# The first product of a second layer by seven half-depth products instead of eight

## The chip, the cores and the metric

One core of one Trainium2 chip. Its engines work side by side, each through its own list of instructions in order: TensorE (PE: matmuls; PEld: its weight loads), VectorE (DVE), ScalarE (ACT), GpSimd (POOL) and SyncE (SP), whose queue issues the DMAs. The metric is the device time of one execution in microseconds (us), lower is better.

## The reference

Pooled attention feeds a gated layer, and that a second layer with the Mish function; everything is float32.

```python
x = attention(q, pool(k), pool(v))                  # 2304 tokens x 512
x = (sigmoid(x @ w_gate) * (x @ w_val)) @ w_out     # 512 -> 1536 -> 512
h = x @ w_in                                        # 512 -> 2048: the product that is changed
g = h * np.tanh(np.log1p(np.exp(h)))                # Mish
return g @ w_out2                                   # 2048 -> 512
```

## The kernel before

Every float32 operand of a matmul is split into a high part (a cast to the matmul's type) and a low part (operand minus high part). A product is then three matmuls: high x high, high x low, low x high (`mm3`, lines 98 to 101). All matmuls accumulate over the depth in PSUM, 128 rows at a time, in eight banks.

The first layer runs over five blocks of 512, 384, 384, 512 and 512 tokens, and in each over twelve pieces `f` of the inner width: `pg`, `pv` (products with the gate and the value weights), sigmoid and multiplication, and one piece later the `acc` matmuls with `wo`. Beside them lie the attention of the next block and the conversion of weights: they come as 64-bit numbers, a ScalarE step and three VectorE steps (`conv_scale` line 137, `conv_bits` lines 146 to 150) make float32 of them, and `conv_parts` casts on ScalarE and subtracts on GpSimd (line 160). `step` and `w2_step` say when. Of the second layer's 32 weight tiles eight are converted early and stored in DRAM as parts (`fin_w2`), 24 in the last block, into the places of first-layer weights that are done. `finish` splits a block's result into parts (lines 513 and 514) and stores both.

The second layer (lines 645 to 708) goes over the same blocks and, in each, over 16 pieces `f` of 128 inner columns. `h_unit` makes `ph` with four depth steps of `mm3` (12 matmuls), then Mish twice on ScalarE (lines 673 and 674: once in float32, once as the high part) and one subtraction on VectorE (line 675). `out_unit` follows two pieces later (`LAG`): for each 128 tokens three matmuls of 512 columns into `acc` (line 689). When a block ends its four or three `acc` banks are copied and stored.

The program's text is the order: each engine gets its instructions as they are written, nothing is rescheduled. An instruction waits by semaphores for its inputs and for the last readers of a tile whose place it takes.

## Time and profile before

| | |
|---|---|
| median of 3 runs | 952.81 us (951.9 to 953.5) |
| the profiled execution | 950.78 us, its span 949.0 us |
| TensorE (PE) busy | 917.7 us, 97% of the span, 4708 matmuls |
| VectorE (DVE) busy | 396.1 us, 42% |
| ScalarE (ACT) busy | 349.0 us, 37% |
| GpSimd (POOL) busy | 142.2 us, 15% |
| chain that ended last | PE 84%, DVE 10%, issue 3%, ACT 1%, DMA 1% |
| mean granted clock of TensorE | 0.991 |
| DMA | 114.04 MB, 120 GB/s over the span |

Busy shares are averages over the span. A matmul's duration in the trace overlaps that of the next, so its pace is the distance of two starts. An idle time is listed before the instruction that ended it, with what released it.

### The profile page before, as it was taken

What the parts mean: (1) busy time and instruction counts of PE and PEld (TensorE: products, weight loads), DVE (VectorE), ACT (ScalarE), POOL (GpSimd) and SP (SyncE); (2) the same over time, 40 slices, a digit from 0 to 9 for tenths busy, and PEclk for the clock granted to TensorE, in tenths of its full rate; (3) what the DMA queues carried; (4) which work ended last, traced back from release to release, by engine and by line L of the source; (5) the groups of instructions that cost most, each with busy time, mean ns of one, the idle gap of its engine ahead of it and who ended that gap; (6) DMA issues with size and microseconds to landing.
All of it is one profiled execution on the core that took longest, in us unless ns stands there. A gap on an engine that the chain in (4) does not pass through costs nothing.

```text
span 949.0 us, 12208 instructions
## 1 busy us (share of the span) xinstructions
PE 917.7 (97%) x4708; PEld 794.1 (84%) x4708; DVE 396.1 (42%) x651; ACT 349.0 (37%) x832; POOL 142.2 (15%) x144
## 2 busy tenths in 40 slices
PE   6889779999999999999999999999999999999998
PEld 6767658999999988888888888888888888999997
DVE  6999996533364343332687741112112111111111
ACT  5644455434355554344443342122122121222221
POOL 5567451020021100000133310000000000000000
PEclk9999899999999999999999999999999999999999
DMA  7577564633474362243765563003002100300000
GB/s 254 166 226 248 178 194 147 205 108 106 169 230 135 123 211 100 89 138 122 275 223 195 179 231 124 1 1 134 1 0 74 37 1 1 112 1 0 34 1 34
DMA packets 39610, 114.04 MB, mean 120 GB/s; under 512 B 4480, under 2 KB 6528, under 8 KB 39552
## 3 DMA queue, kind: packets, MB, share of 16 engines
q1 hardware_dynamic: 39552, 113.26, 35.1%
q8 instruction: 37, 0.61, 0.3%
q14 instruction: 21, 0.17, 0.1%
HBM read 88.60 MB, written 24.64 MB: 119 GB/s over the span
## 4 chain that ended last, share of the span: by engine, by line
PE 84%; DVE 10%; issue 3%; ACT 1%; DMA 1%; SPq 0%; DVEq 0%; ACTq 0%
PE acc L689 21%; PE ph L99 7%; PE ph L101 7%; PE ph L100 7%; PE acc L99 4%; PE acc L100 4%; PE pg L352 4%; PE acc L101 4%; PE pv L352 4%; PE pg L353 4%; PE pg L356 4%; PE pv L353 4%; PE pv L356 4%; DVE cv L147 4%; DVE cv L146 2%
## 5 line engine op out<-in xcount | busy, mean ns | idle before, releaser
L689 PE MATMUL acc<-w,g 128*128 128x512 f32 x864 | 209.8, 390 | 0.0
L689 PEld LDWEIGHTS acc<-w,g 128*128 128x128 f32 x864 | 161.7, 188 | 32.2
L675 DVE TENSOR_TENSOR g<-q,g 128x512 fp32r<-128x512 f32 (+1 forms) x80 | 51.1, 639 | 324.3 <-ACT g L674 324.3
L673 ACT ACTIVATE q<-ph 128x512 f32<-128x512 f32 (+1 forms) x80 | 44.5, 556 | 296.9 <-PE ph L101 296.9
L101 PE MATMUL ph<-x,w 128*128 128x512 f32 (+1 forms) x320 | 117.9, 368 | 0.0
L99 PE MATMUL ph<-x,w 128*128 128x512 f32 (+1 forms) x320 | 117.8, 368 | 0.0
L100 PE MATMUL ph<-x,w 128*128 128x512 f32 (+1 forms) x320 | 117.7, 368 | 0.0
L99 PE MATMUL acc<-gh,wo 128*128 128x512 f32 (+1 forms) x240 | 91.3, 381 | 1.1 <-ACT gh L617 1.1
L100 PE MATMUL acc<-gl,wo 128*128 128x512 f32 (+1 forms) x240 | 89.8, 374 | 2.3 <-POOL gl L489 1.1
L352 PE MATMUL pv<-xh,wv 128*128 128x512 f32 (+1 forms) x232 | 86.9, 375 | 3.8 <-DVE sg L614 3.8
L101 PE MATMUL acc<-gh,wo 128*128 128x512 f32 (+1 forms) x240 | 89.0, 371 | 0.0
L614 DVE TENSOR_TENSOR sg<-sg,pv 128x512 f32<-128x512 f32 (+1 forms) x58 | 36.4, 628 | 125.1 <-PE pv L356 112.2
L352 PE MATMUL pg<-xh,wg 128*128 128x512 f32 (+1 forms) x232 | 87.0, 375 | 0.6 <-ACT sg L608 0.5
L353 PE MATMUL pv<-xl,wv 128*128 128x512 f32 (+1 forms) x232 | 85.6, 369 | 0.0
L353 PE MATMUL pg<-xl,wg 128*128 128x512 f32 (+1 forms) x232 | 85.3, 368 | 0.0
L617 ACT CAST gh<-sg 128x512 fp32r<-128x512 f32 (+1 forms) x60 | 34.7, 578 | 124.7 <-DVE sg L614 124.6
L100 PEld LDWEIGHTS ph<-x,w 128*128 128x128 f32 x320 | 60.1, 188 | 8.9
L150 DVE SCALAR_TENSOR_TENSOR cv<-raw,cv 128x512 uint32<-128x512 uint32 x68 | 66.5, 978 | 2.3
L99 PEld LDWEIGHTS ph<-x,w 128*128 128x128 f32 x320 | 60.1, 188 | 8.8
L101 PEld LDWEIGHTS ph<-x,w 128*128 128x128 f32 x320 | 60.0, 188 | 7.5
L608 ACT ACTIVATE sg<-pg 128x512 f32<-128x512 f32 (+1 forms) x58 | 32.0, 552 | 90.3 <-PE pg L356 90.1
L147 DVE SCALAR_TENSOR_TENSOR cv<-raw,cv 128x512 uint32<-128x512 uint32 x68 | 62.0, 911 | 2.3
(90 smaller groups left out, 1313.1 us busy)
## 6 DMA issues: line engine op xcount, KB each, us to landing
wo<-wod SPq DMA_DIRECT2D x48, 512.0 KB
raw<-w2i SPq DMA_DIRECT2D x16, 512.0 KB
raw<-w2o SPq DMA_DIRECT2D x16, 512.0 KB
raw<-wg SPq DMA_DIRECT2D x12, 512.0 KB
raw<-wv SPq DMA_DIRECT2D x12, 512.0 KB
raw<-wo SPq DMA_DIRECT2D x12, 512.0 KB
wod<-wo SPq DMA_DIRECT2D x12, 512.0 KB
x<-x2d SPq DMA_DIRECT2D x12, 512.0 KB
```

Of the source, the lines that this page charges most:

```text
L99: nc.tensor.matmul(ps, wt[:, 0, cols], xh, start=start, stop=False)
L100: nc.tensor.matmul(ps, wt[:, 0, cols], xl, start=False, stop=False)
L101: nc.tensor.matmul(ps, wt[:, 1, cols], xh, start=False, stop=stop)
L147: nc.vector.scalar_tensor_tensor(out=c, in0=hi, scalar=0x80000000, in1=c, op0=ALU.bitwise_and, op1=ALU.bitwise_or)
L150: nc.vector.scalar_tensor_tensor(out=c, in0=lo, scalar=29, in1=c, op0=ALU.logical_shift_right, op1=ALU.bitwise_or)
L352: nc.tensor.matmul(ps[:, c0:c1], w, xh[:, k, c0:c1], start=(k == 0), stop=False)
L353: nc.tensor.matmul(ps[:, c0:c1], w, xl[:, k, c0:c1], start=False, stop=False)
L356: nc.tensor.matmul(ps[:, c0:c1], w, xh[:, k, c0:c1], start=False, stop=(k == KD - 1))
L614: nc.vector.tensor_mul(out=sg, in0=sg, in1=pv[:, :n])
L673: nc.scalar.activation(out=q, in_=ph[:, :n], func=AF.Mish)
L675: nc.vector.tensor_sub(out=g[:, 1, :], in0=q, in1=f32(g[:, 0, :]))
L689: nc.tensor.matmul(acc[t], g[:, a, c], w[:, b, :], start=(f == 0 and first), stop=(f == NF2 - 1 and last),)
```

## The change

The product `h = x @ w_in` is cut into two by two: the tokens into pairs of groups of 384 (three pairs of 768), the depth of 512 into halves, the inner width into pairs of pieces `f1`, `f2`. Each two by two product, eight half-depth products before, is made by seven (Strassen's scheme in Winograd's form): sums and differences of the x quarters and of the weight quarters are formed first, and the results are combined after.

- `prep_x2` makes, for each token pair and each of two depth steps, seven operands in parts (ScalarE: 7 casts; VectorE: 11 operations of 384 columns). The operands of the next token pair are made in the second half of a token pair, those of the first in the last block of the first layer.
- `prep_w` makes for each weight pair (2 x 512 columns, reloaded from DRAM for every token pair) four weight tiles in parts: 8 operations on VectorE, 4 casts on ScalarE.
- `product` is one of the seven: six matmuls of 384 columns into a PSUM bank, then the sums that read it. Five banks take turns, three hold `acc`.
- Of the four results of a weight pair, two (first token group) go through Mish and `parts` into `out_unit` one weight pair later; two (second group, `g2`) are kept in SBUF, and all sixteen are put through `out_unit` after the loop over weight pairs.
- The spilled weights are the unsplit float32 halves, all 16 `w_in` tiles; their conversion is spread over blocks 3 and 4 (every 4 steps instead of 8), and the 16 tiles of the output weights follow in the last block. `finish` stores x unsplit.

```diff
@@ prep_x2, prep_w
+            return [
+                [hi(1, b11), hi(2, b21)],
+                [lo(1, b11), sub(b11, b12, b11), hi(3, b22), hi(5, b11)],
+                [lo(2, b21), lo(3, b22), sub(b12, b22, b12), hi(7, b12)],
+                [lo(5, b11), sub(b22, b22, b11), hi(6, b22)],
+                [lo(7, b12), sub(b21, b21, b22), hi(4, b21)],
+                [lo(6, b22)],
+                [lo(4, b21)],
+            ]
...
+                    lambda: A.copy(out=w1[:, 0, :], in_=c1),
+                    lambda: V.tensor_sub(out=c2[:, a], in0=c1[:, a], in1=c2[:, a]),
+                    lambda: A.copy(out=w2[:, 0, :], in_=c2),
...
+                    lambda: V.tensor_sub(out=w1[:, 1, :], in0=c1, in1=f32(w1[:, 0, :])),
+                    lambda: V.tensor_sub(out=w2[:, 1, :], in0=c2, in1=f32(w2[:, 0, :])),
+                    lambda: V.tensor_sub(out=h2, in0=h2, in1=c2[:, a]),
+                    lambda: A.copy(out=w4[:, 0, a], in_=h2),
+                    lambda: V.tensor_add(out=c1[:, a], in0=c1[:, a], in1=h2),
+                    lambda: V.tensor_sub(out=c1[:, b], in0=c1[:, b], in1=h2),
+                    lambda: A.copy(out=w3[:, 0, :], in_=c1),
...
+                    lambda: V.tensor_sub(out=w4[:, 1, a], in0=h2, in1=f32(w4[:, 0, a])),
+                    lambda: V.tensor_sub(out=w3[:, 1, :], in0=c1, in1=f32(w3[:, 0, :])),
...
@@ finish, step
-                    nc.scalar.copy(out=xh[:, m, :n], in_=acc[m][:, :n])
-                    nc.vector.tensor_sub(out=xl[:, m, :n], in0=acc[m][:, :n], in1=f32(xh[:, m, :n]))
...
+                    copy((nc.scalar, nc.vector)[m % 2], x, acc[m][:, :n])
...
-                    elif i % 8 == 2 and pos2["c"] < n2:
+                    elif i % 4 == 1 and pos2["c"] < NF2:
...
@@ last block of the first layer
+                    prep = dict(enumerate(prep_x2(0), 7))
...
+                        if k == 15:
+                            load_x2(0, 1)
+                            prep.update(enumerate(prep_x2(1), 18))
...
@@ second layer: parts, the loop over weight pairs
+                    nc.scalar.activation(out=g[:, 0, :], in_=hi_from, func=AF.Mish)
+                    nc.scalar.activation(out=src, in_=hi_from, func=AF.Mish)
+                nc.vector.tensor_sub(out=g[:, 1, :], in0=src, in1=f32(g[:, 0, :]))
...
+                    def product(k, *reads):
+
+                        ps, home = bank(f"p{k}")
+                        part, c0 = PART[k]
+                        for kk in range(2):
+                            xh, xl = top[k, kk]
+                            c = slice(c0 + 128 * kk, c0 + 128 * kk + 128)
+                            mm3(ps[:, :NG], wt[part], c, xh, xl, kk == 0, kk == 1)
+                        for out, in0 in reads:
+                            if in0 is None:
+                                nc.scalar.copy(out=out, in_=ps[:, :NG])
+                            else:
+                                nc.vector.tensor_add(out=out, in0=in0, in1=ps[:, :NG])
+                        banks.append(home)
+
+                    product(1, (a, None))
+                    product(6, (u, a))
+                    product(5, (v, u))
+                    product(7, (g2[f2], v), (u, u))
+                    nc.scalar.activation(out=g2[f2], in_=g2[f2], func=AF.Mish)
+                    if n + 1 < NFP * NPR:
+                        run_all(prep_w(ws_of.pop(n + 1), w_sets[(i + 1) % 2]))
+                        if n + 3 < NFP * NPR:
+                            load_ws(n + 3)
+                    for acc_, f, g in pend:
+                        out_unit(acc_, f, g)
...
+                    product(2, (a, a))
+                    pend.append((acc, f1, parts(a, a)))
+                    product(3, (g2[f1], v))
+                    nc.scalar.activation(out=g2[f1], in_=g2[f1], func=AF.Mish)
+                    product(4, (u, u))
+                    pend.append((acc, f2, parts(u, u)))
...
@@ the second token group of a pair
+                gs = {0: parts(g2[0])}
+                out_unit(acc2, 0, gs.pop(0))
+                for n, (acc_, f, g) in enumerate(pend):
+                    out_unit(acc_, f, g)
+                    gs[n + 1] = parts(g2[n + 1])
+                evict(acc, o)
+                pend = []
+                for f in range(1, NF2):
+                    if p + 1 < NPR and f >= NF2 - 2:
+                        pend.append((acc2, f, gs.pop(f)))
+                    else:
+                        out_unit(acc2, f, gs.pop(f))
+                    if f + 2 < NF2:
+                        gs[f + 2] = parts(g2[f + 2])
```

Three places show how instructions move. VectorE in the second layer, before, where a block ends (`g` is the subtraction after Mish, `ob` a copy of `acc`):

```order
L675 TENSOR_TENSOR g_5545<-q2_5544,g_5545 128x512
L675 TENSOR_TENSOR g_5575<-q2_5574,g_5575 128x512
L700 COPY ob_5594<-acc1_5126 128x512
L700 COPY ob_5600<-acc3_5128 128x512
L675 TENSOR_TENSOR g_5625<-q2_5624,g_5625 128x512
```

and now, inside one weight pair, from `prep_w` (`ws` and `w2s`) to the sum of product 4:

```order
L158 TENSOR_TENSOR ws_5515<-ws_5515 128x256
L162 TENSOR_TENSOR w2s_4946<-ws_5515,w2s_4946 128x512
L163 TENSOR_TENSOR w2s_4947<-ws_5515,w2s_4947 128x512
L164 TENSOR_TENSOR ws_5515<-ws_5515 128x256
L166 TENSOR_TENSOR ws_5515<-ws_5515 128x256
L167 TENSOR_TENSOR ws_5515<-ws_5515 128x256
L171 TENSOR_TENSOR w2s_4949<-ws_5515,w2s_4949 128x256
L172 TENSOR_TENSOR w2s_4948<-ws_5515,w2s_4948 128x512
L826 TENSOR_TENSOR a_5678<-a_5678,p2_5747 128x384
L772 TENSOR_TENSOR g_5755<-a_5678,g_5755 128x384
L826 TENSOR_TENSOR g2_12_5061<-v_5680,p3_5759 128x384
L826 TENSOR_TENSOR u_5679<-u_5679,p4_5768 128x384
```

One subtraction for each piece became 17 operations for each weight pair, the reads of the PSUM banks `p2`, `p3` and `p4` behind the eight of `prep_w`. ScalarE at a block's end, before:

```order
L673 ACTIVATE q2_5574<-ph_5561 128x512
L674 ACTIVATE g_5575<-ph_5561 128x512
L702 COPY ob_5591<-acc0_5125 128x512
L702 COPY ob_5597<-acc2_5127 128x512
L673 ACTIVATE q2_5624<-ph_5611 128x512
```

and now, at the end of the last weight pair of the first token pair (`a` and `u` come from products 2 and 4, `g2_0` is the first kept piece of the second token group):

```order
L770 ACTIVATE g_5857<-a_5780 128x384
L771 ACTIVATE a_5780<-a_5780 128x384
L850 ACTIVATE g2_14_5063<-g2_14_5063 128x384
L770 ACTIVATE g_5878<-u_5781 128x384
L771 ACTIVATE u_5781<-u_5781 128x384
L768 CAST g_5885<-g2_0_5070 128x384
L768 CAST g_5906<-g2_1_5071 128x384
```

The cast of `g2_0`, which the next `acc` matmuls read, stands behind the Mish of the last two results. VectorE in the last block of the first layer, before, between two multiplications `sg` (`cv`: weight conversion):

```order
L614 TENSOR_TENSOR sg_4620<-sg_4620,pv_4632 128x512
L621 TENSOR_TENSOR gl_4647<-sg_4620,gh_4646 128x512
L146 TENSOR_SCALAR cv_4628<-cv_4628 128x512
L147 SCALAR_TENSOR_TENSOR cv_4628<-raw_4591,cv_4628 128x512
L150 SCALAR_TENSOR_TENSOR cv_4628<-raw_4591,cv_4628 128x512
L146 TENSOR_SCALAR cv_4656<-cv_4656 128x512
L147 SCALAR_TENSOR_TENSOR cv_4656<-raw_4630,cv_4656 128x512
L150 SCALAR_TENSOR_TENSOR cv_4656<-raw_4630,cv_4656 128x512
L614 TENSOR_TENSOR sg_4687<-sg_4687,pv_4699 128x512
```

and now, in the third such stretch, up to the second conversion (`st`: loaded x quarters, `top` and `xh1`: operands):

```order
L715 TENSOR_TENSOR sg_4446<-sg_4446,pv_4462 128x512
L722 TENSOR_TENSOR gl_4477<-sg_4446,gh_4476 128x512
L222 TENSOR_SCALAR cv_4454<-cv_4454 128x512
L223 SCALAR_TENSOR_TENSOR cv_4454<-raw_4411,cv_4454 128x512
L226 SCALAR_TENSOR_TENSOR cv_4454<-raw_4411,cv_4454 128x512
L133 TENSOR_TENSOR xh1_96<-st_4193,xh1_96 128x384
L136 TENSOR_TENSOR st_4199<-st_4199,st_4193 128x384
L133 TENSOR_TENSOR top3_4204<-st_4195,top2_4203 128x384
L136 TENSOR_TENSOR st_4197<-st_4197,st_4199 128x384
```

Four subtractions of `prep_x2` now stand between the two conversions.

## Rows read from the trace of the kernel before

**Rows 1.** Busy time, second layer: PE, PEld, DVE, ACT, POOL; granted clock; DMA share; GB/s.
```profile
550.10:945.40 395.30, 395.27 (x1825) 337.49 (x1823) 61.24 (x95) 89.02 (x176) 2.78 (x2) 1.00 0.12 45
```

**Rows 2.** Timeline, TensorE, blocks of 512: start, duration, line, tile, count.
```profile
550.10 0.39 PE L99 MATMUL ph<-x,w 128*128 128x512 f32 x1
...
558.26 2.90 PE L689 MATMUL acc<-w,g 128*128 128x512 f32 x12
```

**Rows 3.** Timeline, TensorE, a unit in a block of 384.
```profile
880.44 2.24 PE L689 MATMUL acc<-w,g 128*128 128x512 f32 x9
...
882.52 0.33 PE L99 MATMUL ph<-x,w 128*128 128x384 f32 x1
...
884.62 2.24 PE L689 MATMUL acc<-w,g 128*128 128x512 f32 x9
```

**Rows 4.** Groups by line and form, TensorE: count, busy us, mean ns.
```profile
L99 PE MATMUL ph<-x,w 128*128 128x512 f32 x192 | 74.7, 389 | 0.0
...
L99 PE MATMUL ph<-x,w 128*128 128x384 f32 x128 | 43.1, 337 | 0.0
```

**Rows 5.** Groups by line and form, VectorE and ScalarE.
```profile
L675 DVE TENSOR_TENSOR g<-q,g 128x384 fp32r<-128x384 f32 x32 | 17.9, 558 | 114.1 <-ACT g L674 114.1
...
L673 ACT ACTIVATE q<-ph 128x384 f32<-128x384 f32 x32 | 15.7, 492 | 104.2 <-PE ph L101 104.2
...
L617 ACT CAST gh<-sg 128x384 fp32r<-128x384 f32 x24 | 12.4, 515 | 43.6 <-DVE sg L614 43.5
...
L91 ACT CAST w<-cv 128x512 fp32r<-128x512 f32 x24 | 14.8, 616 | 5.3 <-DVE cv L150 5.3
...
L673 ACT ACT_TABLE_LOAD x1 | 1.3, 1283 | 0.0
```

**Rows 6.** Timeline, one unit of 384: the last `ph` matmul, ScalarE, VectorE.
```profile
880.26 0.33 PE L101 MATMUL ph<-x,w 128*128 128x384 f32 x1
...
880.63 0.49 ACT L673 ACTIVATE q<-ph 128x384 f32<-128x384 f32 x1 [3.31 <-PE ph L101]
...
881.02 0.49 ACT L674 ACTIVATE g<-ph 128x384 fp32r<-128x384 f32 x1
...
881.54 0.56 DVE L675 TENSOR_TENSOR g<-q,g 128x384 fp32r<-128x384 f32 x1 [3.63 <-ACT g L674]
...
882.03 0.69 DVE L700 COPY ob<-acc 128x512 f32<-128x512 f32 x1
```

**Rows 7.** Timeline, VectorE, four and two alike in a row.
```profile
553.88 2.48 DVE L514 TENSOR_TENSOR xl<-acc,xh 128x512 fp32r<-128x512 f32 x4 [1.22 <-ACT xh L513]
...
163.93 0.76 DVE L308 TENSOR_TENSOR xl<-pv,xh 128x256 fp32r<-128x256 f32 x2 [1.23 <-ACT xh L306]
```

**Rows 8.** Timeline, TensorE after two idle times; idle before in brackets.
```profile
54.95 0.50 PE L352 MATMUL pv<-xh,wv 128*128 128x512 f32 x1 [2.89 <-DVE sg L614]
...
95.62 1.04 PE L282 MATMUL tr<-ident,e 128*72 128x128 f32 x8 [2.00 <-DVE e L273]
```

**Rows 9.** Busy times and granted clock after each (columns as in rows 1).
```profile
56.20:59.60 3.40, 3.40 (x9) 2.63 (x8) 3.40 (x4) 1.55 (x4) 3.04 (x3) 0.50 0.90 289
97.00:98.00 1.00, 1.00 (x6) 0.83 (x5) 0.97 (x3) 0.24 (x1) 0.68 (x1) 1.00 0.00 0
```

**Rows 10.** Timeline, last block of the first layer, VectorE and GpSimd.
```profile
480.65 0.68 DVE L614 TENSOR_TENSOR sg<-sg,pv 128x512 f32<-128x512 f32 x1
...
482.58 1.30 POOL L160 TENSOR_TENSOR w<-cv,w 128x512 fp32r<-128x512 f32 x1 [2.40 <-ACT w L91]
...
482.62 1.53 DVE L146 TENSOR_SCALAR cv<-cv 128x512 uint32<-128x512 uint32 x1
...
485.53 0.42 DVE L146 TENSOR_SCALAR cv<-cv 128x512 uint32<-128x512 uint32 x1
...
488.30 0.68 DVE L614 TENSOR_TENSOR sg<-sg,pv 128x512 f32<-128x512 f32 x1
```

**Rows 11.** The page: busy tenths of VectorE in 40 slices.
```profile
DVE  6999996533364343332687741112112111111111
```

More of the change, by code (lines that the diff above doesn't have):

```diff
@@ new lines, in tile_pooled_attention_moe_mish, with load_ws, run_all @@
+        ws_of = {}
+        def load_ws(i):
+            t = ws_of[i] = wpool.tile([128, 2, 512], F32, tag="wo", name="ws", bufs=NWO)
+            nc.sync.dma_start(out=t, in_=w2d[i % NFP])
+        def run_all(rows):
+            for row in rows:
+                for fn in row:
+                    fn()
+        with ExitStack() as actx:
+            ps_mm = actx.enter_context(
+                tc.tile_pool(name="ps_mm", bufs=2, space=bass.MemoryType.PSUM, reuse_waits="tile")
+            )
+            ps_at = actx.enter_context(
+                tc.tile_pool(name="ps_at", bufs=2, space=bass.MemoryType.PSUM, reuse_waits="tile")
+            )
@@ L687, in out_unit @@
+            def out_unit(acc, f, g):
+                w = w2_t[f]
+                for t in range(NTG):
                     c = slice(128 * t, 128 * t + 128)
@@ L706, in tile_pooled_attention_moe_mish, with evict @@
-            for u in range(NU + LAG):
-                if u < NU:
-                    j, f = units[u]
-                    if f == 2 and b_order.index(j) + 1 < NBLK:
-                        load_x2(b_order[b_order.index(j) + 1])
-                    h_unit(u)
-                if u >= LAG:
-                    out_unit(u - LAG)
+            def evict(acc, o):
+                for t in range(NTG):
+                    ps, home = acc[t]
+                    ob = pb.tile([128, 512], F32, tag="ob", name="ob", bufs=3)
+                    copy((nc.scalar, nc.vector)[t % 2], ob, ps)
+                    nc.sync.dma_start(out=out[o + 128 * t : o + 128 * t + 128, :], in_=ob)
+                    banks.append(home)
@@ L719 @@
+            evict(acc2, o + NG)
 def kernel(**inputs):
```

209 lines of the change are left out of this document (132 added, 77 removed).

## The prediction

> **What bounds the kernel now.** Read first the shares of busy time in the table ahead: TensorE 97%. Then the busy time of one stretch, the second layer: from its first `ph` matmul at 550.10 us to 945.4 us TensorE is busy 395.27 of 395.30 us, at a granted clock of 1.00, with VectorE at 61.24 and ScalarE at 89.02 us [rows 1]. So nothing is waited for there but TensorE: columns taken out of its stream are time won, and any wait that the change puts into that stream is paid in full. TensorE's pace is read from the distance of starts in its timeline, not from the duration of one matmul, which overlaps the next. 36 `ph` matmuls of 512 columns start between 550.10 and 558.26 us: 0.2267 us each; 12 `acc` matmuls of 512 take (2.90 - 0.39)/11 = 0.228 us each [rows 2]. In a block of 384 tokens nine `acc` matmuls last from 880.44 to 882.52 us (0.231 us each), twelve `ph` matmuls of 384 columns to 884.62 us (0.175 us each) [rows 3].
>
> **Matmuls removed and added.** Each of the three lines of `mm3` issues 192 `ph` matmuls of 512 columns and 128 of 384 [rows 4]: 576 x 0.2267 + 384 x 0.175 = 197.8 us. The change issues 3 token pairs x 8 weight pairs x 7 products x 6 = 1008 matmuls of 384 columns, 48 more than before, with an eighth fewer columns: 1008 x 0.175 = 176.4 us. The 864 `acc` matmuls stay, but all in nines: 864 x 0.231 = 199.6 against 576 x 0.228 + 288 x 0.231 = 197.9 us. Sum: -21.4 + 1.7 = **-19.7 us**.
>
> The Trainium skill (TensorE: Matmul & The Clock Gate, Back-to-back issue gap) gives the spacing of matmuls as N/2.4 ns + 2.5 ns, thus 162.5 ns for 384 columns. By an estimate from that page the products would save 22.9 us and the `acc` matmuls change nothing; the rows show 175 ns, and the measurement decides.
>
> **What the scheme needs from VectorE and ScalarE.** Before, a unit asks two Mish (0.49 us) and one subtraction (0.56 us) [rows 5]. Now one weight pair (18 `acc` and 42 product matmuls, 18 x 0.231 + 42 x 0.175 = 11.5 us of TensorE) asks VectorE for 9 operations of 384 columns, 3 of 512 and 5 of 256, and ScalarE for 11, in an order in which each waits for the other. Distances of starts on VectorE: 0.49 us at 384 (881.54 to 882.03) [rows 6]; at 512 and 256, (2.48 - 0.68)/3 = 0.60 and 0.76 - 0.42 = 0.34 us [rows 7]. Sum: 9 x 0.48 + 3 x 0.60 + 5 x 0.34 = 7.8 us. A handover costs 0.03 to 0.04 us (TensorE's end at 880.59, ScalarE's start at 880.63) [rows 6]. VectorE's waits, laid out by hand: before a `sub` it waits for two Mish in a row on ScalarE, the second of which overwrites what the first reads; 2 x 0.51 + 3 x 0.04 + the rest of its own last operation = 1.2 us, and this twice; three waits for casts of weight parts (0.62 us for 512 columns [rows 5]), 0.9 us; three sums that use the one before, 0.3 us. Together 3.6, so the chain needs **11.4 us per weight pair beside TensorE's 11.5**. Mish out of SBUF is not in the trace; I take the cast of the same width out of SBUF (0.515 us [rows 5]), bounds 0.49 and 0.62. So inside the loop I count no wait, with 0.1 us to spare; what is over that is rival 2.
>
> Four places where TensorE waits nevertheless:
> - The first weight pair has no `acc` matmuls beside it. After product 7 TensorE has only products 2, 3, 4 and the next 1, 6, 5 (6 x 1.05 = 6.3 us) before the next product 7, whose PSUM bank is that of product 3. VectorE reads product 3 as the 13th of its chain, 8.1 us after it began, and ScalarE first loads the Mish table, 1.28 us [rows 5]: 0.2 + 8.1 + 1.3 + 0.2 (waking TensorE) = 9.8 us. **+3.5 us**, bounds 2 and 5.
> - After the eighth weight pair of each token pair, TensorE has products 3 and 4 (2.1 us) and then the `acc` matmuls of `g2[0]`, whose cast stands behind the five Mish of the last two halves on ScalarE. From product 2: 0.2 + add 0.56 + two Mish 1.1 + `sub`, sum, sum 1.5 + two Mish 1.0 + cast 0.5 + waking 0.2 + handovers 0.1 = 5.2 us, less 2.1; then 0.2 for the low part: 3.3 us, three times, and in the first token pair about 1.1 us more, left over from the table load. **+11.0 us**, bounds 8 and 15.
> - Clock. After an idle time of 2.89 us (start 54.95 us) TensorE runs from 56.2 to 59.6 us at a granted clock of 0.50, i.e. 1.2 GHz; after one of 2.00 us (start 95.62 us) the clock stays at 1.00 [rows 8, 9]. 3.4 us at half the clock lose 1.7 us. The three waits at the ends are 3.3 to 4.4 us, nearer to the first row: **+5.1 us**, bounds 0 and 5.
> - Last block of the first layer. VectorE is nearly full there: 7.65 us from `sg` to `sg` (480.65 to 488.30) [rows 10], against TensorE's 8.16 (36 x 0.2267). The change puts 22 subtractions among them, at most 5, 5, 1, 0, 7, 4 between two `sg` in turn, 0.48 us each: VectorE falls 1.9, 3.8, 3.8, 3.3 and then over 5 us behind. A `pv` product can be read late by 5.4 us (one `acc` and one `pg` step) less 1.1 for the read and the waking, 4.3; beyond that TensorE waits. **+1.5 us**, bounds 0 and 4.
>
> The rows show what GpSimd does to VectorE here: `cv` L146 takes 1.53 us while GpSimd's 1.30 us subtraction runs, and 0.42 without it [rows 10], 1.1 us more per GpSimd operation. The Trainium skill (SBUF — State Buffer, Who interferes with whom) says that a VectorE operation with two SBUF inputs and a GpSimd one that reads SBUF exclude each other for the whole instruction, and the added subtractions have two such inputs. The 16 GpSimd operations left in that block (24 before) would by that hold VectorE 0.2 us longer each, 3 us in all, and the term would be about 3 us instead of 1.5.
>
> Hidden: eight more weight conversions in the third and fourth block, where VectorE is at 2 to 6 tenths (slices 12 to 19) [rows 11]; the 512 KB reload of every weight pair, two pairs ahead, beside a DMA share of 0.12 [rows 1]; the preparation of the next token pair, beside the 28 us of `acc` matmuls that follow each loop; one copy instead of cast and subtraction in `finish`, a little less than before. If the preparation lost its cover it would show as a wait before product 1.
>
> **Sum.** -19.7 + 3.5 + 11.0 + 5.1 + 1.5 = +1.4 us on the profiled execution's 950.78 us (its span of 949.0 and 1.8 around it). That execution lies 2.0 us below the median of the runs; I put the difference on the median: 952.8 + 1.4 = **954.2 us**. About 0.2% (1.9 us) is what a measurement here can tell from no change.
>
> **Rivals.**
> 1. The waits cost less: the clock holds (-5.1), the last block hides its work (-1.5), and the ends wait 9 us (-2). Sum -7, about 946 us. For it: the row with 2.00 us held the clock, and VectorE's 7.65 us in the last block are less than TensorE's 8.16. Against: 2.89 us lost it.
> 2. The VectorE-ScalarE chain is longer than TensorE's 11.5 us per weight pair and becomes the bound of the loop. It decides from 1% more than worked out. Every 0.1 us over costs about 23 x 0.1 = 2.3 us, since a lag inside the loop is paid at its end. 5% longer (11.98): 0.46 x 23 = 10.6 us, about 964 us; 10%: 24 us, about 977 us. For it: handovers, in-place Mish and 256-column operations are unseen in this arrangement. Against: all pieces come from rows, rounded up.
> 3. The change doesn't do what it says: matmuls of 384 columns, changing weights each time, lose their pace without the `acc` matmuls of 512 between. At the 512 pace per column (0.2267/512 x 384 = 0.170) nothing is lost; at 0.19 us, 15 us, thus 969 us. Rows 3 show 0.175 over twelve in a row, so this is unlikely.
>
> **Chances.** Forecast, 950 to 957 us: 0.38. Rival 1, 943 to 950: 0.32. Rival 2, above 957: 0.26. Rival 3: 0.04. Faster by over 0.2% (below 950.9): 0.32 + 0.04 of the forecast = 0.36. Slower (above 954.7): 0.26 + 0.04 + 0.11 = 0.41. The rest, 0.23, is no change. The range leaves out a tenth at each end: 944 to 964 us, down to most of rival 1 and up to rival 2 at 5%.
>
> **What would show it.** TensorE's `p` matmuls of 384 should start 0.175 us apart, 42 of them and 18 `acc` in 11.5 us. Idle time before the first `acc` matmul of each second half: about 3 us, put down to ScalarE's cast, with a clock of 0.50 after it. Idle time in the first weight pair: 3 to 4 us, put down to VectorE. `pv` of the last block should wait for `sg` a little. If weight pairs in the middle of the loop take 12 us and TensorE waits there for VectorE, rival 2 was right; if no idle time shows at the ends, the forecast was wrong.

## The result

The changed kernel took 963.73 us (median of 4 runs, 963.26 to 965.16) where the kernel before took 952.37 us (4 runs): a ratio of 1.012, with a 95% interval of 1.0103 to 1.0138. It is slower by 11.4 us. The forecast was 954.2 us: the time lies inside the range, 0.3 us from its edge, and outside the 950 to 957 us of the likeliest case. One execution of a later run, e11_adds_first, took 2055.81 us; its ratio leaves it out.

The profiled execution took 963.39 us, its span 961.6 us (949.0 before). First the second layer, as one stretch of the windows view; it answers to [rows 1].

```profile
561.50:957.90 396.40, 381.49 (x1873) 340.35 (x1871) 249.09 (x499) 172.98 (x349) 0.00 (x0) 0.98 0.15 50
```

It starts at 561.50 us instead of 550.10, and takes 396.4 us instead of 395.3. So of the 12.6 us by which the two spans differ, 11.4 were lost ahead of the layer that the change is about. In that layer TensorE is now busy for 381.5 us instead of 395.3, and the other 14.9 us are waits, so that what the scheme saves there is spent again; the mean clock is 0.98, and VectorE does 249 us of work instead of 61. Then TensorE's matmul groups of the page: what kept each waiting stands behind the bar.

```profile
L780 PE MATMUL acc<-w,g 128*128 128x512 f32 x864 | 206.9, 398 | 12.7 <-ACT g L768 12.7
...
L428 PE MATMUL pg<-xh,wg 128*128 128x512 f32 (+1 forms) x232 | 87.8, 379 | 7.6 <-ACT sg L709 7.5
...
L428 PE MATMUL pv<-xh,wv 128*128 128x512 f32 (+1 forms) x232 | 87.0, 375 | 5.6 <-DVE sg L715 5.6
...
L99 PE MATMUL p<-top,w2s 128*128 128x384 f32 x216 | 73.4, 340 | 1.4 <-DVE g L826 0.8
```

The 12.7 us are three waits in the second layer; 7.6 us fall on the first layer's `pg`, which waits for ScalarE's sigmoid. (Most of the 5.6 us of `pv` lie before 130 us, where the kernel before waits too.) TensorE's timeline says where (idle time before the instruction in brackets):

```profile
267.14 0.44 PE L428 MATMUL pg<-xh,wg 128*128 128x384 f32 x1 [3.23 <-ACT sg L709]
...
361.50 0.50 PE L428 MATMUL pg<-xh,wg 128*128 128x512 f32 x1 [0.82 <-ACT sg L709]
...
497.32 0.50 PE L428 MATMUL pg<-xh,wg 128*128 128x512 f32 x1 [1.37 <-ACT sg L709]
...
523.86 0.50 PE L428 MATMUL pg<-xh,wg 128*128 128x512 f32 x1 [1.53 <-ACT sg L709]
...
571.11 0.44 PE L99 MATMUL p<-top,w2s 128*128 128x384 f32 x1 [0.54 <-ACT w2s L165]
573.40 0.41 PE L99 MATMUL p<-xh,w2s 128*128 128x384 f32 x1 [0.62 <-DVE a L826]
575.53 0.45 PE L99 MATMUL p<-top,w2s 128*128 128x384 f32 x1 [0.82 <-DVE g L826]
...
658.96 1.65 PE L780 MATMUL acc<-w,g 128*128 128x512 f32 x3 [5.01 <-ACT g L768]
...
790.70 9.61 PE L780 MATMUL acc<-w,g 128*128 128x512 f32 x35 [5.01 <-ACT g L768]
...
919.17 1.40 PE L780 MATMUL acc<-w,g 128*128 128x512 f32 x3 [2.71 <-ACT g L768]
```

Four places, then: the third and fourth block of the first layer, its last block, the first weight pair (TensorE stands at the second one's products, for weight parts and bank reads that the first still owes), and the ends of the three token pairs. After each of these last the clock is at 0.50 for some us, as after the first idle time in [rows 8, 9]; in windows of 1 us:

```profile
658.00:659.00 1.00, 0.04 (x1) 0.04 (x1) 0.46 (x1) 1.00 (x3) 0.00 (x0) 0.50 0.00 0
...
663.00:664.00 1.00, 1.00 (x4) 0.81 (x3) 0.25 (x1) 0.51 (x1) 0.00 (x0) 0.54 0.00 0
...
792.00:793.00 1.00, 1.00 (x4) 0.71 (x4) 0.00 (x0) 0.00 (x0) 0.00 (x0) 0.50 0.00 0
...
922.00:923.00 1.00, 1.00 (x4) 0.73 (x3) 0.00 (x0) 0.00 (x0) 0.00 (x0) 0.50 0.00 0
```

The pace, against [rows 2, 3], is read from the distance between weight pairs: here the starts of product 2 in two neighbours of the first token pair, and in two of the second.

```profile
604.19 0.33 PE L99 MATMUL p<-xl,w2s 128*128 128x384 f32 x1
...
615.81 0.33 PE L99 MATMUL p<-xl,w2s 128*128 128x384 f32 x1
...
713.81 0.33 PE L99 MATMUL p<-xl,w2s 128*128 128x384 f32 x1
...
725.23 0.33 PE L99 MATMUL p<-xl,w2s 128*128 128x384 f32 x1
```

11.42 us is TensorE's own pace (18 `acc` matmuls at 0.229 us and 42 product matmuls at 0.174). The first token pair runs at 11.6 us, though the timeline lists no idle time there after the first weight pair. VectorE, at 1 tenth in the second layer before [rows 11], is now mostly at 6 or 7 until the last two slices (from the page):

```profile
DVE  7999995432365444432698547774677765677631
```

### The profile page after: what moved, and what is told of

It reads as the page before. It is cut to its first block, busy times and chain, and to the rows that moved or that the text cites. A ratio compares the mean times of both kernels' runs of the same rounds, so it can differ in the third digit from the quotient of the medians.

```text
span 961.6 us, 12866 instructions
## 1 busy us (share of the span) xinstructions
PE 906.8 (94%) x4756; PEld 796.5 (83%) x4756; DVE 594.8 (62%) x1081; ACT 430.3 (45%) x1002; POOL 120.7 (13%) x128
## 4 chain that ended last, share of the span: by engine, by line
PE 56%; DVE 25%; ACT 11%; issue 6%; DMA 2%; SPq 0%; DVEq 0%; ACTq 0%
PE acc L780 15%; DVE cv L223 4%; PE pg L428 4%; PE acc L99 3%; PE pv L428 3%; PE pv L429 3%; PE acc L100 3%; PE pv L432 3%; PE acc L101 3%; PE pg L429 3%; PE pg L432 3%; DVE cv L222 3%; PE p L101 2%; PE p L99 2%; PE p L100 2%
## 5 line engine op out<-in xcount | busy, mean ns | idle before, releaser
L780 PE MATMUL acc<-w,g 128*128 128x512 f32 x864 | 206.9, 398 | 12.7 <-ACT g L768 12.7
L780 PEld LDWEIGHTS acc<-w,g 128*128 128x128 f32 x864 | 165.3, 192 | 48.2 <-ACT g L768 13.7
L428 PE MATMUL pg<-xh,wg 128*128 128x512 f32 (+1 forms) x232 | 87.8, 379 | 7.6 <-ACT sg L709 7.5
L428 PE MATMUL pv<-xh,wv 128*128 128x512 f32 (+1 forms) x232 | 87.0, 375 | 5.6 <-DVE sg L715 5.6
L99 PE MATMUL p<-top,w2s 128*128 128x384 f32 x216 | 73.4, 340 | 1.4 <-DVE g L826 0.8
L101 PE MATMUL p<-top,w2s 128*128 128x384 f32 x216 | 72.6, 336 | 0.1
L100 PE MATMUL p<-top,w2s 128*128 128x384 f32 x216 | 72.3, 335 | 0.0
L432 PE MATMUL pg<-xh,wg 128*128 128x512 f32 (+1 forms) x232 | 57.6, 370 | 0.0
L428 PEld LDWEIGHTS pg<-xh,wg 128*128 128x128 f32 x232 | 43.7, 188 | 16.4 <-ACT sg L709 10.1
L432 PE MATMUL pv<-xh,wv 128*128 128x512 f32 (+1 forms) x232 | 56.9, 366 | 0.0
L772 DVE TENSOR_TENSOR g<-g,g 128x384 fp32r<-128x384 f32 x48 | 26.0, 556 | 47.1 <-ACT g L768 47.1
L428 PEld LDWEIGHTS pv<-xh,wv 128*128 128x128 f32 x232 | 43.6, 188 | 13.5 <-DVE sg L715 8.0
```

The lines of the kernel that those rows point to most:

```text
L99: nc.tensor.matmul(ps, wt[:, 0, cols], xh, start=start, stop=False)
L100: nc.tensor.matmul(ps, wt[:, 0, cols], xl, start=False, stop=False)
L101: nc.tensor.matmul(ps, wt[:, 1, cols], xh, start=False, stop=stop)
L428: nc.tensor.matmul(ps[:, c0:c1], w, xh[:, k, c0:c1], start=(k == 0), stop=False)
L432: nc.tensor.matmul(ps[:, c0:c1], w, xh[:, k, c0:c1], start=False, stop=(k == KD - 1))
L780: nc.tensor.matmul(acc[t][0], g[:, a, c], w[:, b, :], start=(f == 0 and first), stop=(f == NF2 - 1 and last),)
```

## The experiments

Each is the changed kernel with one edit, unless it says otherwise. Ratios are to the kernel before on the same chip; the changed kernel's is 1.012. Where a single profile is compared, the second layer's start is good to about 1 us: five kernels with the same first layer start it between 560.8 and 563.1 us.

**The copies of `finish`.** The timeline of ScalarE in the changed kernel, third block of the first layer:

```profile
256.29 0.45 ACT L91 COPY xs<-acc 128x384 f32<-128x384 f32 x1
...
260.96 0.48 ACT L91 COPY xs<-acc 128x384 f32<-128x384 f32 x1 [4.23 <-DMA x2d<-xs]
261.46 1.28 ACT L335 ACT_TABLE_LOAD   x1
```

The second copy waits for a store of the first. Both use the one `raw` buffer that the conversions leave free.

```diff
+            xs_pool = actx.enter_context(tc.tile_pool(name="xsp", bufs=1, reuse_waits="tile"))
...
-                    if m % 2 == 0:
+                    if m == 0 and n < NB:
+                        t = xs_pool.tile([128, 2, 384], F32, tag="xs", name="xs", bufs=1)
+                    elif m % 2 == 0:
                         t = pa.tile([128, 2, 512], F32, tag="raw", name="xs", bufs=3)
```

> The changed kernel, but in `finish` of the two 384-token blocks the first pair of copies gets a buffer of its own (3 KB per partition) instead of one of the three of tag `raw`; everything else stays. Theory: in the third and fourth block both pairs of copies fell on the one `raw` buffer that the running conversions leave free, so the second pair waits for the store of the first (4.23 and 3.42 us of idle time on ScalarE at 260.96 and 355.22 us, releaser x2d<-xs), and everything behind it on ScalarE, the sigmoid of the next `pg` above all, is late. It expects that wait under 0.5 us, TensorE's waits at 267 and 361 us gone, the second layer's first product about 5.5 us earlier (556 instead of 561.5 us) and about 958.2 us instead of 963.7, a ratio to the kernel before of 1.006. Rival: the conversions, one every fourth step instead of every eighth, fill ScalarE and VectorE in these blocks, and the wait is only where it shows; it expects under 1 us, 963 us, ratio 1.011 to 1.012.

Measured: 960.18 us, ratio 1.009 (1.0076 to 1.0103). ScalarE's two copies now:

```profile
257.79 0.47 ACT L91 COPY xs<-acc 128x384 f32<-128x384 f32 x1
258.71 0.48 ACT L91 COPY xs<-acc 128x384 f32<-128x384 f32 x1 [0.45 <-PE acc L101]
```

The wait for the store is gone, so are TensorE's at 267 and 361 us, and the second layer starts at 556.86 us, 4.6 us earlier. By the ratios the gain is 2.9 us: the profiled execution was the fastest of its four. The theory holds, smaller than expected; the rival (the conversions themselves) would have left the waits in place.

**The last block.** Here ScalarE stands at casts that wait for VectorE, and the sigmoid is behind them. Is it their order, or VectorE's amount of work?

```diff
-                [lo(1, b11), sub(b11, b12, b11), hi(3, b22), hi(5, b11)],
-                [lo(2, b21), lo(3, b22), sub(b12, b22, b12), hi(7, b12)],
+                [lo(1, b11), sub(b11, b12, b11), hi(3, b22)],
+                [lo(2, b21), lo(3, b22), sub(b12, b22, b12), hi(5, b11)],
...
```

> The changed kernel, but in `prep_x2` each ScalarE cast that reads a difference made by VectorE is issued one step (2.7 us) after that difference instead of in the same step; the same 22 subtractions stay on VectorE at the same steps. Theory: in the last block of the first layer ScalarE stands at such a cast until VectorE has worked through a weight conversion (3.51 us at 495.32, 3.22 at 521.39, 3.50 at 532.44 us, releaser st<-st), and the sigmoid behind it frees the bank of the next `pg` late. It expects those three waits under 1.5 us each, TensorE's waits before `pg` at 497.3, 523.9 and 533.5 us mostly gone, 3 to 5 us in all: about 959.5 us, ratio 1.0075. Rival (the step of the forecast): VectorE itself has too much in this block, and what is late is its read of `pv`; as its work is the same, it expects under 1 us: 963 us, ratio 1.011 to 1.012.

Measured: 964.51 us, ratio 1.0135 (1.0121 to 1.0149): no gain. TensorE's two clearest waits in that block:

```profile
498.94 0.50 PE L428 MATMUL pg<-xh,wg 128*128 128x512 f32 x1 [0.43 <-ACT sg L709]
...
529.62 0.50 PE L428 MATMUL pv<-xh,wv 128*128 128x512 f32 x1 [1.66 <-DVE sg L715]
```

`pg` waits less (1.13 us in all, 3.43 in the changed kernel), `pv` more (2.69 instead of 0.72), together 3.82 us instead of 4.15. My theory fell: the casts were only where it showed. From the wait at 361 us (364.06 here) to the second layer's start it is 199.8 us, 200.0 in the changed kernel. What did not change is how late VectorE reads `pv`. The worst case in the changed kernel, the last four matmuls of a `pv` product and VectorE's read of it:

```profile
518.54 1.07 PE L432 MATMUL pv<-xh,wv 128*128 128x512 f32 x4
...
526.52 0.67 DVE L715 TENSOR_TENSOR sg<-sg,pv 128x512 f32<-128x512 f32 x1
```

That is 6.9 us behind the product's end; two other reads there come 6.3 and 5.9 us behind, and in e2 the same three 6.9, 6.2 and 5.9. So the work itself was moved, to the steps where the conversions have ended (with e2's order of the casts):

```diff
-                    prep = dict(enumerate(prep_x2(0), 7))
+                    rows = prep_x2(0)
+                    prep = {22: rows[0], 23: rows[1], 24: rows[2], 25: rows[3] + rows[4], 26: rows[5] + rows[6]}
...
-                        if k == 15:
+                        if k == 27:
                             load_x2(0, 1)
-                            prep.update(enumerate(prep_x2(1), 18))
+                            prep.update(enumerate(prep_x2(1), 29))
...
```

> The changed kernel, but the 22 subtractions and 14 casts of the first token pair's `x2` parts stand in the last third of the first layer's last block (steps 22 to 35 instead of 7 to 24), behind the weight conversions, with each cast one step after the difference that it reads. Theory after e2_casts_later (whose waits only moved from ScalarE's `sg` to VectorE's: 3.82 instead of 4.17 us): VectorE itself has more work in the steps with conversions than TensorE's time there. It expects the waits of that block (4.17 us between 497 and 537 us) to go, about 5 us less, as the block also lost some to shorter waits: 959 us, ratio 1.007. Rival: the work is only late elsewhere, the parts of the second half of `x2` come after 561 us and the second layer's first products wait 2 to 5 us: 962 to 964 us, ratio 1.010 to 1.0125.

Measured: 958.14 us, ratio 1.0067 (1.0052 to 1.0081). TensorE's timeline lists no idle time between 362 us and the second layer, which starts 5.4 us earlier, counted from the wait at 361.47 us (194.6 us instead of 200.0):

```profile
556.05 0.33 PE L99 MATMUL p<-xl,w2s 128*128 128x384 f32 x1
```

Then GpSimd's part in VectorE's load:

```diff
                     t = w2_t[f] = wpool.tile([128, 2, 512], F32R, tag="w", name=f"w2_{f}", bufs=2 * NF)
-                    conv_parts(t)
+                    conv_parts(t, (nc.scalar, nc.vector))
```

> The changed kernel, but in the last block of the first layer the low part of each of the 16 converted weights is taken on VectorE (0.69 us) instead of GpSimd (1.30 us). Theory: each GpSimd subtraction holds a VectorE operation for 1.1 us longer (L222 1.54 instead of 0.42, L133 1.65 instead of 0.55 us), so VectorE has less to do without it, 16 x (1.1 - 0.61) = 8 us, and falls less behind: most of the 4.2 us of waits in that block go, 3 to 5 us less: 959.5 us, ratio 1.0075. Rival: the longer rows are of other origin; VectorE then has 16 x 0.61 = 10 us more and TensorE waits 3 to 8 us more: 967 to 972 us, ratio 1.0155 to 1.0205.

Measured: 966.0 us, ratio 1.015 (1.0135 to 1.0165). One conversion step and one kind of the new subtractions in that block, shortest, median and longest in ns; first in the changed kernel:

```profile
L222 DVE TENSOR_SCALAR cv<-cv x15: 416/422/1541, 468.7 to 532.8; 128x512 uint32<-128x512 uint32 x15
...
L133 DVE TENSOR_TENSOR top<-st,top x9: 550/552/1652, 495.2 to 534.6; 128x384 fp32r<-128x384 f32 x9
```

and without GpSimd's subtractions:

```profile
L222 DVE TENSOR_SCALAR cv<-cv x15: 418/420/422, 471.7 to 537.2; 128x512 uint32<-128x512 uint32 x15
...
L133 DVE TENSOR_TENSOR top<-st,top x9: 549/551/553, 497.2 to 539.0; 128x384 fp32r<-128x384 f32 x9
```

The hold is GpSimd's: without it no such row is longer than 422 or 553 ns. It lasts until GpSimd is through, as this pair of the changed kernel shows:

```profile
524.39 1.31 POOL L236 TENSOR_TENSOR w<-cv,w 128x512 fp32r<-128x512 f32 x1 [5.83 <-ACT w L91]
524.47 1.65 DVE L133 TENSOR_TENSOR top<-st,top 128x384 fp32r<-128x384 f32 x1
```

GpSimd's subtraction ends at 525.70 us, VectorE's 0.4 us later. But the time did not follow. VectorE now does a subtraction that must wait for ScalarE's cast, and all its work stands behind it; from VectorE's timeline:

```profile
499.83 0.69 DVE L236 TENSOR_TENSOR w<-cv,w 128x512 fp32r<-128x512 f32 x1 [1.58 <-ACT w L91]
```

From 487 to 545 us there are six such waits, 6.8 us together. The stretch after the wait at 361 us (362.90 here) is 1.9 us longer. Both sides were wrong on the size: the hold was gone, but the new waits cost more than that was worth.

**The token-pair ends.**

```diff
+                    if i == NFP - 2:
+                        for f in range(2):
+                            gs[f] = pb.tile([128, 2, NG], F32R, tag="g", name="g", bufs=4)
+                            nc.scalar.copy(out=gs[f][:, 0, :], in_=g2[f])
...
                     product(2, (a, a))
+                    if i == NFP - 2:
+                        for f in range(2):
+                            nc.vector.tensor_sub(out=gs[f][:, 1, :], in0=g2[f], in1=f32(gs[f][:, 0, :]))
...
-                gs = {0: parts(g2[0])}
-                out_unit(acc2, 0, gs.pop(0))
+                for f in range(2):
+                    out_unit(acc2, f, gs.pop(f))
...
```

> The changed kernel, but the two parts of `g2[0]` and `g2[1]` are made in the seventh weight pair of each token pair, in a pause of VectorE, and TensorE runs both their `acc` matmuls (18) before those of the last two first halves; the number of operations stays. Theory: the waits at the three token-pair ends (5.01, 5.01 and 2.71 us of idle time) come from the order alone, the cast of `g2[0]` standing behind five Mish, and the clock at 0.50 after them (to 664, 794 and 923 us) from the idle time alone. It expects idle time before the first `acc` matmul of a second half under 0.5 us, a clock of 1.00 throughout, and 12.7 us of waits plus about 4.9 us of clock less: about 946 us, ratio 0.993. Rival A: the VectorE and ScalarE chain is behind at the end whatever the order, so the wait moves to the `acc` matmuls of the last two halves: 3 to 5 us less, about 959 us, ratio 1.007. Rival B: waits go but the clock falls elsewhere (another cause than idleness): 951 us, ratio 0.9985.

Measured: 947.69 us, ratio 0.9962 (0.9948 to 0.9976): 15 us less, faster than the kernel before. No wait at an end is left and the clock stays at 1.00 (first window); a small one appears later, twice (second fence, timeline):

```profile
658.00:660.00 2.00, 2.00 (x11) 1.65 (x10) 1.48 (x3) 1.30 (x3) 0.00 (x0) 1.00 0.00 0
```

```profile
673.05 2.25 PE L780 MATMUL acc<-w,g 128*128 128x512 f32 x8 [0.72 <-ACT g L768]
```

So the waits came from the order, and the clock from the waits. Why were the first two 5 us and not the 3.3 of the forecast?

```diff
-                    if n + 1 < NFP * NPR:
+                    if n + 1 < NFP * NPR and i < NFP - 1:
                         run_all(prep_w(ws_of.pop(n + 1), w_sets[(i + 1) % 2]))
...
+                if p + 1 < NPR:
+                    run_all(prep_w(ws_of.pop(NFP * p + NFP), w_sets[0]))
                 evict(acc, o)
```

> The changed kernel, but after the eighth weight pair of the first and the second token pair the next weight pair's preparation (8 operations of VectorE, 4 of ScalarE) stands behind the parts of `g2[0]` to `g2[2]` instead of ahead of the read of product 2. Theory: the first two ends wait 5.01 us and the third 2.71 because only the first two have that preparation on VectorE ahead of the read (the read starts at 654.22, when the preparation ends, 2.3 us after product 2; at the third end at once). It expects 2.7 to 2.9 us of idle time at all three ends, 2 x 2.3 us and some clock less: about 958.5 us, ratio 1.0065. Rival: the lag comes from the whole chain over eight weight pairs; the wait shortens by under 1 us each: 962 us, ratio 1.0105.

Measured: 959.73 us, ratio 1.0086 (1.0073 to 1.01). All three ends now wait 2.71 us, as expected, but the clock still falls after each:

```profile
656.85 13.46 PE L780 MATMUL acc<-w,g 128*128 128x512 f32 x51 [2.71 <-ACT g L768]
```

```profile
657.00:658.00 1.00, 1.00 (x3) 0.75 (x4) 0.92 (x2) 0.21 (x1) 0.00 (x0) 0.50 0.00 0
```

The 144 `acc` matmuls behind the first two waits take 34.9 and 35.0 us, and 33.0 where the clock holds (e11 below). The waits got shorter and the clock's price did not, which is why the gain stayed under the 5 us expected.

**The first weight pair.** Table load and the second weight pair's parts ahead of the second layer; the load of that pair into a `raw` buffer.

```diff
-                        if k == 33:
-                            load_ws(1)
+                        if k == 34:
+                            nc.scalar.activation(out=gap[:, 1:2], in_=gap[:, 0:1], func=AF.Mish)
+                        if k == 29:
+                            ws = pa.tile([128, 2, 512], F32, tag="raw", name="ws", bufs=3)
...
             emit_out(pj, pf, pgh, pgl, acc_of[pj], pn)
+            run_all(prep_w(ws_of.pop(1), w_sets[1]))
             finish(pj, acc_of.pop(pj), pn)
...
```

> The changed kernel, but ScalarE loads the Mish table in the last block of the first layer (one Mish of one column after its last sigmoid), and the second weight pair's parts are made before the second layer starts instead of in its first weight pair. Theory: the first weight pair has no `acc` matmuls beside it and waits for a chain of VectorE that holds 5 us of weight preparation and the 1.28 us table load; its products 2, 3 and 4 take 2.2 us each instead of 1.04. It expects them at 1.04 to 1.1 us and about 3.5 us less: 960.2 us, ratio 1.0082. Rival: the chain is late from the reads of the products alone; only the table load counts, 1.3 us: 962.4 us, ratio 1.0105.

Measured: 961.83 us, ratio 1.0106 (1.0092 to 1.0119). The three waits went and another came: ScalarE's first read of a product, in its timeline:

```profile
567.47 0.48 ACT L829 COPY a<-p 128x384 f32<-128x384 f32 x1 [4.16 <-DMA x2d<-xs]
```

The new `raw` buffer had pushed the copies of `finish` to the one that lies under `a`. With that load in its old place and the Mish one step earlier (`prep_w` stays ahead of `finish`):

```diff
                         if k == 33:
+                            nc.scalar.activation(out=gap[:, 1:2], in_=gap[:, 0:1], func=AF.Mish)
                             load_ws(1)
...
```

> As e4b_table_w1, but the second weight pair's load keeps its place and buffer, so that the copies of `finish` keep theirs, and the table load stands right behind the last sigmoid. Theory after e4b_table_w1 (whose gain was lost to a new wait: ScalarE's first copy `a` came 4.16 us late, behind the stores of `xs`, whose buffer lies under `a`): with that buffer as before, the first weight pair's wait of about 3.6 us goes: 960.1 us, ratio 1.008. Rival: the stores of `xs` are late in any order that puts weight preparation ahead of `finish`, and the wait comes again, 1 to 2 us: 962 us, ratio 1.0105.

Measured: 957.98 us, ratio 1.0062 (1.0041 to 1.0083). From the first product to the second `product 2`:

```profile
561.01 0.33 PE L99 MATMUL p<-xl,w2s 128*128 128x384 f32 x1
...
576.59 0.33 PE L99 MATMUL p<-xl,w2s 128*128 128x384 f32 x1
```

15.58 us, where the changed kernel takes 19.33 (561.50 to 580.83): 3.75 us. And the following weight pairs take 11.43 us, so the first token pair wins 1.2 us more. In the changed kernel the lag from the first wait had never been made up.

**How near the chain is to being the bound.**

```diff
                     product(7, (g2[f2], v), (u, u))
+                    nc.vector.tensor_tensor(out=v, in0=v, in1=v, op=ALU.max)
```

> The changed kernel with one more VectorE operation in each of the 24 weight pairs, a maximum of `v` with itself (384 columns, about 0.48 us, value unchanged), behind the reads of product 7. It measures how much the chain of VectorE and ScalarE has to spare against TensorE's 11.43 us per weight pair. By the forecast (0.1 us to spare) each weight pair is 0.38 us longer, about 8.7 us in all: 972 us, ratio 1.021. By the trace of the changed kernel, where VectorE still waits 0.17 us twice per weight pair for TensorE's products (648.05 and 648.71 us), 0.34 us are to spare: 0.14 x 23 = 3.2 us: 967 us, ratio 1.0155. If over 0.5 us are to spare (VectorE's waits for Mish hide the operation): 964 us, ratio 1.012.

Measured: 969.84 us, ratio 1.0192 (1.0172 to 1.0212). Two neighbours in the first token pair, and one of TensorE's many small waits in between:

```profile
594.41 0.33 PE L99 MATMUL p<-xl,w2s 128*128 128x384 f32 x1
...
601.00 0.45 PE L99 MATMUL p<-top,w2s 128*128 128x384 f32 x1 [0.15 <-DVE g L826]
...
606.27 0.33 PE L99 MATMUL p<-xl,w2s 128*128 128x384 f32 x1
```

11.86 us instead of 11.62: the loop follows VectorE, and half of the operation's 0.48 us is paid in each weight pair. The time lies between the first two expectations. In the second token pair the weight pairs take 11.43 us three times and 11.9 from the fourth on, in the third likewise: VectorE's lag grows unseen as long as there is time to spare from the token pair's start, and TensorE feels it when that is used up. Over a whole token pair there was next to nothing to spare. Then the same work in a better order:

```diff
-                nc.vector.tensor_sub(out=g[:, 1, :], in0=src, in1=f32(g[:, 0, :]))
+                fn = lambda: nc.vector.tensor_sub(out=g[:, 1, :], in0=src, in1=f32(g[:, 0, :]))
+                fn() if low is None else low.append(fn)
...
-                    pend.append((acc, f1, parts(a, a)))
+                    low = []
+                    pend.append((acc, f1, parts(a, a, low)))
                     product(3, (g2[f1], v))
...
-                    pend.append((acc, f2, parts(u, u)))
+                    pend.append((acc, f2, parts(u, u, low)))
+                    for fn in low:
+                        fn()
```

> The changed kernel, but in each weight pair VectorE does the two sums with products 3 and 4 before the two low parts, in the 1.15 us in which it now waits for two Mish; the operations are the same. Theory: the loop of VectorE and ScalarE takes 11.61 us per weight pair against TensorE's 11.43 (the first token pair runs at 11.60 to 11.64; e7_one_more_op at 11.86 to 11.90) and this takes about 1.0 us out of it. It expects all weight pairs at 11.43 us (1.3 us less in the first token pair) and the three ends about 1 us shorter, with 0.5 us of clock each: 4 to 6 us less, 958.5 us, ratio 1.0065. Rival: TensorE's handovers set the 11.6 us, not the sum of VectorE's operations and waits: no weight pair gets shorter, at most 1 us from the ends: 963 us, ratio 1.011.

Measured: 951.84 us, ratio 1.0001 (0.9989 to 1.0014): twice what was expected. All weight pairs take 11.43 us. The ends wait 2.16 us (timeline), and the clock holds (window):

```profile
653.01 17.28 PE L781 MATMUL acc<-w,g 128*128 128x512 f32 x74 [2.16 <-ACT g L768]
```

```profile
654.00:655.00 1.00, 1.00 (x6) 0.82 (x5) 0.08 (x1) 0.00 (x0) 0.00 (x0) 1.00 0.09 16
```

In the profiled execution the ends give back 6.2 us of waits and 4.9 of clock, the loop and the first weight pair 2.4. That is 13.5 us, where the ratios say 11.3: it was the fastest of its executions, and whether the clock held in the others too isn't shown. I had underrated the clock and the ends: VectorE, no longer behind when it comes out of `prep_w`, reads product 2 at 649.12 us, 0.5 us after its end, where it was 2.5 us late. The first two ends, with `prep_w` ahead of that read, now wait no longer than the third without it: it costs nothing where VectorE comes to it without a lag.

**Together.** First four edits (e1, e3, e5, e6), with the parts of `g2` made three ahead instead of two:

```diff
-                    if f + 2 < NF2:
-                        gs[f + 2] = parts(g2[f + 2])
+                    for nf in range(f + 2 if f == 2 else f + 3, min(f + 4, NF2)):
+                        gs[nf] = parts(g2[nf])
```

> All that has helped so far together: own buffer for the copies (e1_own_copies), early halves at the token-pair ends (e3_early_halves) with the parts of `g2` made three instead of two ahead, `x2` parts behind the conversions (as e5_x2_after_conv), table and second weight pair early (as e6_table_w1). If the losses are independent: 963.7 - 4.7 - 16 - 1.4 - 5 - 3.6 = 933 us, ratio 0.980. If time that is won ahead of a wait is partly lost again in another (the waits share VectorE): 940 us, ratio 0.988. If the first layer's gain doesn't reach the end: 947 us, ratio 0.9955.

Measured: 930.54 us, ratio 0.9776 (0.9759 to 0.9793). No loss hid in another: a little more came back than the expected sum. With e11's order added:

> e8_all together with the order of e11_adds_first: VectorE does the sums with products 3 and 4 before the two low parts. In e8_all no wait at a token-pair end is left, but the first token pair and the end of the second still run at 11.50 to 11.66 us per weight pair instead of 11.43, 1.3 us in all. If the chain of VectorE and ScalarE is the cause, as e11_adds_first showed for the changed kernel, all weight pairs take 11.43 us: 929.2 us, ratio 0.976. The 11 us that the order brought alone came from the ends and their clock, which are already gone here. Rival: the parts of `g2` made early in the seventh weight pair need the pause in which the sums now stand, and the loop is late again: 930.5 us or more, ratio 0.9776 or more.

Measured: 929.08 us, ratio 0.9767 (0.9752 to 0.9781); its interval overlaps that of e8_all, but the trace shows what was expected, all weight pairs at 11.43 us. The second layer starts here:

```profile
551.20 0.33 PE L99 MATMUL p<-xl,w2s 128*128 128x384 f32 x1
```

and the only idle time that TensorE's timeline lists from 150 us to the end is 0.35 us, at 340 us. The kernel before has 0.53 us there, so it had no such waits to win back. So the scheme itself is worth 2.3%, and the changed kernel lost that, and 1.2% more, by its order and by one buffer too few.

## Why the prediction was right or wrong

The forecast summed to +1.4 us; it was +11.4. That the time still fell inside the range is luck: its upper end, 964 us, was set by rival 2 at a chain 5% longer, while 8.5 of the 10 us that were missing come from the first layer, from one term put too small and one put at nothing. By its own terms:

- **Matmuls, -19.7 us: right, slightly too small.** 24 weight pairs at 11.43 us and the other 432 `acc` matmuls at 0.227 (in e12, with no wait ahead, 144 start within 32.45 us) make 372.3 us against 395.3: -23.0. An `acc` matmul in nines, 0.229 us in the weight pairs, costs no more than in twelves. For the products the 0.174 us of the loop stand by the row. The Trainium skill (TensorE: Matmul & The Clock Gate, Back-to-back issue gap) gives 162.5 ns, for a matmul on its own and not for a stream with weight loads; this trace doesn't agree with it as the pace of a stream.
- **First weight pair, +3.5: right, by the path that was named.** 3.75 us (e6). The second pair's product 7 starts at 575.53 us, 9.8 us after the first pair's ended, put down to VectorE's read of product 3.
- **Ends, +11.0: the size off.** 12.7 us. The step that failed: it let VectorE read product 2 as soon as that ended. Of the first two ends, 2.3 us each are `prep_w` standing ahead of that read (e9) in a chain that is already late (e11); the last, without it, waits 2.71 us instead of 3.3. The 1.1 us more for the first token pair did not show, 5.01 us at both; without the early lag the first end waits 4.50 us (e6), so the lag was worth about 0.5.
- **Clock, +5.1: right in this execution.** 4.9 us: the matmuls behind the three ends take 2.1, 1.2 and 1.6 us longer than in e11. (There the first three behind each wait still start 0.33 us apart, 0.3 us per end that e12 doesn't have.) But the argument, a wait near 2.89 us loses the clock and one of 2.00 keeps it, does not hold: see the last section. The third end, 2.71 us here, kept its clock in e2, e5 and e7.
- **The loop counted at no wait: nearly.** The chain was put at 11.4 us and TensorE at 11.5; they are 11.6 and 11.43. (The sum took 0.48 us for an operation of 384 columns where its row gave 0.49; with that, the 0.1 us to spare were gone.) Rival 2 was thus true in its mechanism, though small: 1.2 us in the first token pair, and in the other two the lag stayed within the spare time until the eighth pair. But e11 shows that this lag also lengthened the ends, so its whole cost was larger than what the loop shows.
- **Last block, +1.5 (0 to 4): too small.** 5.4 us (e5). The mechanism was the one named, VectorE's overload; the step that failed is its sum. By its own figures the lag is 6.15 us in the fifth stretch (3.3 + 7 x 0.48 - 0.51) and, after a wait of 1.85, 5.7 in the sixth: 3.3 us beyond the 4.3 us allowed, not 1.5. Measured, the reads of `pv` come 6.3, 6.9 and 5.9 us late, so the lag itself was larger; why isn't separated. That TensorE waits mostly at `pg`, behind ScalarE's casts, and not at `pv` as forecast, is only where it shows (e2). The Trainium skill (SBUF — State Buffer, Who interferes with whom) says that a VectorE operation with two SBUF inputs and a GpSimd one that reads SBUF exclude each other for the whole instruction, and the trace agrees: VectorE's subtraction ends 0.4 us after GpSimd's. But the hold on the new subtractions is then the same 1.1 us as on the conversions (1.65 against 0.55 us for L133), and not 0.2 us longer as was worked out for a term of 3 us.
- **`finish` "a little less than before", 0: wrong, 4.6 us (e1).** The step counted operations and not buffers. Two more users of three `raw` buffers made a copy wait for a store in front of ScalarE's whole queue. This, with the 3.9 us more in the last block, is most of what separates +1.4 from +11.4. The reloads and the next token pair's preparation did stay hidden: no wait before a product 1 is listed.

These terms make -23.0 + 3.75 + 12.7 + 4.9 + 0.9 (the slower first matmuls behind the three waits) + 1.2 + 5.4 + 4.6, about +10.5 us; the two spans differ by 12.6. Of the 2 us left, 1.4 lie in the first layer (11.4 less 4.6 and 5.4), about as much as its start varies; they stay open.

Rival 1 (946 us) fell in all three parts: the clock dropped, the last block cost 5.4 us, the ends waited 12.7. Rival 3 fell with 0.174 us per matmul.

## What to carry to other kernels

When a change takes a tile from a pool that something else already uses, count the tiles alive at that place, and price the wait of whatever in-order queue the copy stands in. A chain that needs as long as the bounding engine gives no slack for a single late start: order its operations so that each pause of one engine holds work whose inputs are ready, before cutting anything. And remove a wait of the matmul engine rather than shorten it: at 2.71 us instead of 5.01 it still cost the clock in eight cases of eleven, and then about as much.

## What the runs showed of the hardware that was not expected

- The length of an idle time alone does not say whether TensorE's clock falls. At the ends of token pairs it fell to 0.50 after every wait of 4.5 us or more and stayed at 1.00 after 2.16 us (three times, e11). After 2.71 us it fell in eight cases, among them all three ends of e9, and stayed at 1.00 in three (e2, e5, e7). Here the third end of e5, wait and clock, and below it e12 at the place where the kernel before kept its clock after 2.00 us [rows 8, 9]:

```profile
914.44 15.92 PE L782 MATMUL acc<-w,g 128*128 128x512 f32 x68 [2.71 <-ACT g L770]
915.00:916.00 1.00, 1.00 (x5) 0.76 (x5) 0.52 (x2) 0.00 (x0) 0.00 (x0) 1.00 0.00 0
...
95.34 1.31 PE L358 MATMUL tr<-ident,e 128*72 128x128 f32 x8 [2.00 <-DVE e L349]
97.00:98.00 1.00, 1.00 (x4) 0.81 (x3) 1.00 (x2) 0.00 (x0) 0.96 (x1) 0.50 0.00 0
```

In the kernel before it also fell after 1.90 us (27.57 us). What decides between the two isn't shown. A longer wait did not cost more clock in proportion: against e11 the matmuls behind waits of 4.5 us or more took 1.2 to 2.6 us longer in all these runs, those behind a fall after 2.71 us 1.6 to 2.0 us.

- A 1.30 us subtraction on GpSimd lengthens a VectorE operation that starts beside it by 1.1 us whether that reads one or two tiles (L222 0.42 to 1.54, L133 0.55 to 1.65): VectorE ends 0.3 to 0.4 us after GpSimd. Without GpSimd the longest of 15 was 422 ns.
